# Attention and two MLPs on one core: transposes side by side, value products a step later, the exponentials' scale from a register

## The chip, the core and the metric

The kernel runs on one core of a Trainium2 chip. The core's engines run side by side, each through its own list of instructions in the order in which the program gives them: TensorE (PE in the profile; its weight loads are PEld), VectorE (DVE), ScalarE (ACT), GpSimd (POOL), and the queue on SyncE (SP) that issues most DMAs. They wait for each other by semaphores alone. The metric is the device time of one execution, in microseconds (us); all times below are us unless marked ns.

## The reference

What is computed is an attention over 2 batches, 12 heads, 448 positions and 64 dimensions per head, with the scores capped, and then two MLPs over the 896 tokens:

```python
scores = scale * np.matmul(q, k.transpose(0, 1, 3, 2))
scores = cap * np.tanh(scores / cap)
scores = scores - np.max(scores, axis=-1, keepdims=True)
attn = np.exp(scores)
attn = attn / (np.sum(attn, axis=-1, keepdims=True) + 1e-09)
out = np.matmul(attn, v)
# x: [896, 768] from out; then twice x = g(x @ w_in) @ w_out, 768 -> 2048 -> 768,
# g is ELU in the first MLP and leaky ReLU in the second
```

All is float32, and cap is an input (30).

## The kernel before, in words

**Two stages.** The attention works on 12 pairs of heads (n = 0 to 11), one pair after the other. The MLPs follow: products of 128x448 tiles, L655 (into the hidden layer) and L763 (out of it), each float32 product made of three with operands split into a rounded part and a remainder. The weights of the MLPs come in by DMA in a raw form and are converted on ACT and DVE (L564 to L594), then split (L304 on ACT, L307 on DVE). The first weights are converted while the attention still runs.

**One pair.** SP loads the pair's keys, queries and values (nk, nq, nv, L331). PE transposes keys and queries (L349, four products with the identity each, into PSUM tiles ntk and ntq), and DVE copies them out (kT, L367; qT with the scale 1/(8 cap), L363). PE makes the scores in four chunks of 112 keys (sc n.0 to n.3, L380, both heads of a chunk at once, in two halves of the array's rows). ACT takes tanh of each chunk (L400) and then the exponential of two chunks at a time, in place (e n.0 and e n.1, 112x1792, L408). POOL adds the two chunks of each half (s n.0, s n.1, L417), and DVE adds the halves (L423). PE multiplies this by ones (sm, L519), so that the sums of the softmax stand in every row, and the exponentials by the values in four chunks (po, L505, the two heads in two halves of the array's columns). DVE takes the reciprocal of the sums (rec, L525) and multiplies (xf, L533); ACT rounds xf (xh, L304), DVE takes the remainder (xl, L307), and both go into the first MLP.

**The exponential before** has two operands that are a column of 128 numbers in SBUF: the scale capb (the cap) and the bias nbound (minus its absolute value). The sums divide the bias out again. There is a second form of the block for large caps (row_softmax); a branch chooses at the start, and with this cap the first form runs.

**Buffers.** PSUM has eight banks: two score buffers of two banks (tag sc), one for transposes (nt), two for the products with the values (po, later also for the MLPs' accumulators), one for the sums (sm). Before the change ntk and ntq of every pair share the one nt buffer, apart from the first queries, which take sm.

**What sets the order.** Nothing is ordered by hand. Each step is put down with an engine, an assumed cost, what it reads and writes, and a wished or due time (`plan(...)`). The class `Plan` then plays the program through with these costs and writes down an order for each engine; PE pays `SWITCH` in that play when the kind of its work changes (transpose, scores, attend, MLP), and keeps to a kind a while. The order that comes out is fixed at build time. TP is the length that the plan assumes for one pair, and the wished times are multiples of it.

Of the kernel before, what the change touches and what calls it, by code (L numbers as in the profile page):

```python
# [23 lines left out]
class Plan:  # L24
# [10 lines left out]
    LANDING = 2.0  # L35
    AHEAD = 60.0
    STAY = 2.0
    SWITCH = 0.12

    def __init__(self, capacity):  # L40
        self.ops = []
# [151 lines left out]
@with_exitstack  # L193
def attention_elu_mlp_leaky_mlp(
    ctx: ExitStack,
    tc: tile.TileContext,
    q: bass.AP,
    k: bass.AP,
    v: bass.AP,
    cap: bass.AP,  # L200
    w_in1: bass.AP,
    w_out1: bass.AP,
    w_in2: bass.AP,
    w_out2: bass.AP,
    out: bass.AP,
):

    nc = tc.nc
    const = ctx.enter_context(tc.tile_pool(name="const", bufs=1))
    P, D = 128, q.shape[3]
    capb = const.tile([P, 1], F32, name="capb")
    nc.gpsimd.dma_start(out=capb, in_=cap.rearrange("(o n) -> o n", o=1).to_broadcast([P, 1]))

    first = {}
    for nm, src in (("k", k), ("q", q)):
        first[nm] = const.tile([src.shape[2] // 4, 4, 2, D], F32, name=f"first{nm}")  # L230
        nc.sync.dma_start(out=first[nm], in_=src[0, 0:2].rearrange("j (p c) d -> p c j d", c=4))

    busy = const.tile([P, P], F32, name="busy")
    nc.vector.memset(busy, 0.0)
    with tc.tile_pool(name="early", bufs=1, space=PSUM) as early:
        t = early.tile([P, P], F32, name="unused")
        for _ in range(IDLE_PRODUCTS):
            nc.tensor.matmul(t, busy, busy, start=True, stop=True)  # L238
    ident = const.tile([P, P], F32, name="ident")
    make_identity(nc, ident)  # L240
    ones = const.tile([P, D], F32, name="ones")
    nc.gpsimd.memset(ones, 1.0)
    third = const.tile([P, 1], F32, name="third")
    nc.vector.memset(third, -15.5 / 32.0)  # L244
    bits = nc.values_load(cap.bitcast(I32).rearrange("(o n) -> o n", o=1))
    ncap, nbound, qscale = (const.tile([P, 1], F32, name=x) for x in ("ncap", "nbound", "qscale"))
    scratch = const.tile([P, 1], F32, name="scratch")
    consts = dict(busy=busy, first=first, scratch=scratch, third=third, ident=ident, ones=ones, ncap=ncap, capb=capb, nbound=nbound, qscale=qscale)
    args = (tc, consts, q, k, v, w_in1, w_out1, w_in2, w_out2, out)
    with tc.If((bits & 0x7FFFFFFF) <= CAP_BOUND_BITS, preferred_fallthrough_block=True) as small:  # L250
        block(*args, bounded=True)
    with small.Else():
        block(*args, bounded=False)
# [3 lines left out]
def block(ctx, tc, consts, q, k, v, w_in1, w_out1, w_in2, w_out2, out, bounded):  # L257
# [49 lines left out]
        nc.vector.tensor_tensor(out=lo, in0=x, in1=hi.bitcast(F32), op=SUB)  # L307


    TP = 9.0  # L310
    NPAIR = len(order)
    TM = (NPAIR + 0.6) * TP

# [26 lines left out]
    def transpose_nat(nm, n, at):  # L340

        name, pt = f"{nm}T{n}", f"nt{nm}{n}"

        tag = "sm" if n == 0 and nm == "q" else "nt"

        def fn():
            t = tl("ps", tag, pt, [P, 512])
# [23 lines left out]
    def scores(n, c, at):  # L371
# [4 lines left out]
        def fn():  # L376
            t = tl("ps", "sc", name, [P, 2, 512])
            for j in range(2):
# [5 lines left out]
                    start=True, stop=True,  # L384
                )

        plan("PE", 0.93, fn, reads=[f"qT{n}", f"kT{n}"], writes=[(name, 0), (name, 1)],
             new={name: "sc"}, at=at, att=True, kind="scores")

    def half(n, h):  # L390
# [2 lines left out]
    def bounded_softmax(n):  # L393
        for c in range(NC):
# [10 lines left out]
                continue  # L405

            def exponent(name=name):
                nc.scalar.activation(V[name], V[name], AF.Exp, scale=capb[:CP], bias=nbound[:CP])  # L408

            plan("ACT", 1.8, exponent, reads=[(name, 0), (name, 1)],  # L410
                 writes=[(name, 0), (name, 1)], att=True)

            s = f"s{n}.{h}"
# [84 lines left out]
    def attend(n, c, at):  # L498
        po, e = f"po{n}", half(n, c // 2)

        def fn():
            if c == 0:
                tl("ps", "po", po, [P, 512])
            for j in range(2):
                nc.tensor.matmul(  # L505
                    V[po][j * D : (j + 1) * D, :S], V[f"nv{n}"][:, j, c], V[e][:, c % 2, j],
                    start=(c == 0), stop=(c == NC - 1),
                )

        plan("PE", 0.74, fn, reads=[(e, c % 2), f"nv{n}"], writes=[po],  # L510
             new={po: "po"} if c == 0 else None, at=at, att=True, kind="attend")

    def sums(n, at):
# [7 lines left out]
                    start=True, stop=True,  # L521
                )

        plan("PE", 0.74, fn, reads=[f"s{n}.0"], writes=[sm], new={sm: "sm"}, at=at, att=True, kind="attend")
        plan("DVE", 2.97, lambda: nc.vector.reciprocal(out=tl("att", "rec", rec, [P, S]), in_=V[sm][:, :S]),  # L525
             reads=[sm], writes=[rec], new={rec: "rec"}, att=True, due=at + 5)

# [367 lines left out]


    plan("ACT", 1.5, lambda: nc.scalar.activation(scratch, third, AF.Tanh), due=0.0)
    for n in range(NPAIR):
        T = (n + 0.3) * TP
        load("k", k, n)  # L900
        load("q", q, n)
        load("v", v, n)
        transpose_nat("k", n, T - 0.95 * TP)
        transpose_nat("q", n, T - 0.8 * TP)
        if n == 0:

            plan("PE", 0.4, lambda: idle_products("unusedq", 2), writes=["unusedq"], new={"unusedq": "po"},
                 at=T - 0.7 * TP, att=True)
        for c in range(NC):
            scores(n, c, T + c * TP / 4)  # L910
        (bounded_softmax if bounded else row_softmax)(n)
        for c in range(NC):
            attend(n, c, T + (c + 3.6) * TP / 4)
        if bounded:
            sums(n, T + 7.4 * TP / 4)
        x1(n, T + 2.6 * TP)
    TH = 6 * KM * MM
    TO = 3 * MS * (KF // 2) * MM
    T0 = TM
# [59 lines left out]
```

## Time and profile before

| | us |
|---|---|
| median of three runs (557.18 to 558.18) | 557.83 |
| the profiled execution, its own time | 557.47 |
| its span, first to last instruction | 555.6 |
| PE busy in it | 545.6 (98%) |
| DVE busy | 468.9 (84%) |
| ACT busy | 383.6 (69%) |
| POOL busy | 52.7 (9%) |
| attention, to the last product of sums | about 0 to 115 |
| MLPs | about 107 to 555 |

The profiled execution gives the durations; its own time is 557.47, of which 1.87 lie outside the span. A busy PE is not a PE at its peak: matmuls overlap, so the start of one matmul to the start of the next tells more than the duration of one. In the same way two neighbours on ACT or DVE overlap by some 0.1, and the step from start to start is what counts in a row of them. The chain of waits cuts the span into pieces that follow each other, and for these it gives what each cost. The granted clock of TensorE is 1.00 (2.4 GHz) in every stretch of the attention.

### The profile page before, as it was taken

The page shows a single profiled execution, that of the slowest core. Times are in us where ns is not written, and L with a number is a line of the kernel's source. Part 1 is how long each engine was busy: PE and PEld are TensorE (multiplying, and loading weights), DVE is VectorE, ACT ScalarE, POOL GpSimd, SP SyncE. Part 2 cuts the span into 40 slices and gives each one's busy share as a digit, 9 for nine tenths or more (in the row PEclk, how much of TensorE's full clock was granted, in tenths as well). Part 3 has the DMA queues.
Part 4 walks back from the last instruction along what each step waited for, and adds up shares of the span by engine and source line. Part 5 has one row for each costly group of instructions (what it writes and reads, how often), then busy time and mean ns, then how long its engine had stood idle before and what let it go on. Part 6 is the DMA issues. An engine that isn't in the chain of part 4 may idle for free.

```text
span 555.6 us, 7392 instructions
## 1 busy us (share of the span) xinstructions
PE 545.6 (98%) x2756; PEld 452.8 (81%) x2756; DVE 468.9 (84%) x606; ACT 383.6 (69%) x547; POOL 52.7 (9%) x32
## 2 busy tenths in 40 slices
PE   8999999999999999999999999999999999999995
PEld 5333333479999999999999999999999999999994
DVE  2699999996987899899999978987896499998662
ACT  5899999918977788865657757776665256665551
POOL 2554454500000000000000000000000000000000
PEclk9999999999999999999999999999999999999998
DMA  8833551145777677400012136677662000001112
GB/s 165 240 82 83 134 138 42 59 126 166 228 221 221 177 202 227 138 2 1 1 51 63 57 114 207 196 223 221 188 203 70 0 2 0 2 0 51 51 34 71
DMA packets 61434, 61.88 MB, mean 111 GB/s; under 512 B 23248, under 2 KB 53200, under 8 KB 61392
## 3 DMA queue, kind: packets, MB, share of 16 engines
q1 hardware_dynamic: 61120, 61.23, 38.8%
q8 instruction: 23, 0.38, 0.3%
q14 instruction: 19, 0.16, 0.1%
q10 hardware_dynamic: 240, 0.11, 0.1%
q0 software_dynamic: 32, 0.00, 0.0%
HBM read 58.59 MB, written 2.75 MB: 110 GB/s over the span
## 4 chain that ended last, share of the span: by engine, by line
PE 88%; DVE 5%; POOL 2%; ACT 2%; issue 2%; DVEq 0%; POOLq 0%; ACTq 0%
PE acc L655 29%; PE acc L763 24%; PE acs L763 12%; PE po L505 3%; DVE rec L525 2%; PE sm L519 1%; PE ct L848 1%; PE acs34.0_3866 L655 1%; PE acs31.0_3678 L655 1%; PE acs25.0_3299 L655 1%; PE acs22.0_3101 L655 1%; PE acs15.1_1848 L655 1%; PE acs12.1_1645 L655 1%; PE acs6.1_1253 L655 1%; PE acs28.1_3492 L655 1%
## 5 line engine op out<-in xcount | busy, mean ns | idle before, releaser
L525 DVE RECIPROCAL rec<-sm 128x448 f32<-128x448 f32 x12 | 35.4, 2954 | 2.2 <-PE sm L519 2.1
L367 DVE COPY kT<-ntk 128x448 f32<-128x448 f32 x12 | 7.4, 619 | 7.1 <-PE ntk L349 7.0
L349 PEld LDWEIGHTS ntq<-ident,nq 112*128 112x128 f32 x44 | 4.3, 140 | 9.3 <-DVE kT L367 8.6
L349 PEld LDWEIGHTS ntk<-ident,nk 112*128 112x128 f32 x44 | 4.3, 140 | 7.3 <-issue 6.7
L363 DVE TENSOR_SCALAR qT<-ntq,qscale 128x448 f32<-128x448 f32 x12 | 8.2, 679 | 1.5 <-PE ntq L349 1.5
L349 PE MATMUL ntq<-ident,nq 112*128 112x112 f32 x44 | 6.6, 273 | 1.4 <-DVE kT L367 1.4
L533 DVE TENSOR_TENSOR xf<-po,rec 128x448 f32<-128x448 f32 x12 | 7.5, 623 | 0.4
L576 ACT ACTIVATE rawo1.00.2_977<-rawo1.00.2_977 128x768 int32<-128x768 uint8 x1 | 0.9, 937 | 8.6 <-DMA rawo1.00.2_977<-in_moe_w_out_dram 8.6
L349 PE MATMUL ntk<-ident,nk 112*128 112x112 f32 x44 | 6.6, 273 | 0.0
L868 ACT COPY ob<-ct 112x512 f32<-112x512 f32 x7 | 4.1, 587 | 0.5
L238 PE MATMUL unused<-busy 128*128 128x128 f32 x14 | 3.4, 433 | 1.1 <-DVE third L244 1.1
L684 ACT ACTIVATE ea2.14.0_3936<-acs34.0_3866 128x448 f32<-128x448 f32 x1 | 0.5, 545 | 5.3 <-PE acs34.0_3866 L655 5.3
L832 ACT COPY c2.01.0_4934<-acc 128x448 f32<-128x448 f32 x1 | 0.5, 532 | 5.2 <-PE acc L763 5.2
L238 PEld LDWEIGHTS unused<-busy 128*128 128x128 f32 x14 | 3.1, 330 | 1.1 <-DVE third L244 1.1
L687 DVE TENSOR_TENSOR gg2.14.0_3940<-ea2.14.0_3936,acs34.0_3866 128x448 f32<-128x448 f32 x1 | 0.6, 622 | 3.9 <-ACT ea2.14.0_3936 L684 3.9
L834 DVE COPY c2.01.1_4942<-acc 128x448 f32<-128x448 f32 x1 | 0.6, 625 | 3.7 <-ACT c2.01.0_4934 L832 3.7
L307 DVE TENSOR_TENSOR tl2.1.3_3986<-gg2.3.0_3266,th2.1.3_3984 128x448 fp32r<-128x448 f32 x1 | 0.6, 624 | 3.6 <-PE acs L763 3.6
L304 ACT CAST th2.1.3_3984<-gg2.3.0_3266 128x448 fp32r<-128x448 f32 x1 | 0.6, 567 | 4.5 <-PE acs L763 4.5
L400 ACT ACTIVATE e0.0_160<-sc0.0_152 112x896 f32<-112x896 f32 x1 | 0.9, 919 | 3.9 <-PE sc0.0_152 L380 3.9
L669 ACT ACTIVATE ea1.0.0_1067<-acc 128x448 f32<-128x448 f32 x1 | 0.5, 546 | 4.4 <-PE acc L655 4.4
L675 DVE SCALAR_TENSOR_TENSOR gg1.0.0_1079<-ea1.0.0_1067,acc 128x448 f32<-128x448 f32 x1 | 0.6, 624 | 3.4 <-ACT ea1.0.0_1067 L672 3.4
L684 ACT ACTIVATE ea2.13.0_3886<-acc 128x448 f32<-128x448 f32 x1 | 0.5, 545 | 3.9 <-PE acc L655 3.9
(4966 smaller groups left out, 2237.2 us busy)
## 6 DMA issues: line engine op xcount, KB each, us to landing
nv<-in_v_dram SPq DMA_DIRECT2D x12, 224.0 KB, 2.9
nk<-in_k_dram SPq DMA_DIRECT2D x11, 224.0 KB, 3.2
nq<-in_q_dram SPq DMA_DIRECT2D x11, 224.0 KB, 3.9
out_dram<-ob SPq DMA_DIRECT2D x3, 672.0 KB, 4.4
rawg1.0_208<-in_moe_w_in_dram SPq DMA_DIRECT2D x1, 768.0 KB, 6.3
rawg1.1_253<-in_moe_w_in_dram SPq DMA_DIRECT2D x1, 768.0 KB, 5.9
rawg1.2_287<-in_moe_w_in_dram SPq DMA_DIRECT2D x1, 768.0 KB, 6.4
rawo1.00.0_519<-in_moe_w_out_dram SPq DMA_DIRECT2D x1, 768.0 KB, 5.5
```

Source lines behind the costliest of these rows:

```text
L238: nc.tensor.matmul(t, busy, busy, start=True, stop=True)
L349: nc.tensor.matmul(t[:, c * CP : (c + 1) * CP], V[f"n{nm}{n}"][:, c], ident[:CP, :CP], is_transpose=True, start=True, stop=True,)
L363: nc.vector.tensor_scalar(out=t, in0=V[pt][:, :S], scalar1=qscale, scalar2=None, op0=ALU.mult)
L367: nc.vector.tensor_copy(t, V[pt][:, :S])
L505: nc.tensor.matmul(V[po][j * D : (j + 1) * D, :S], V[f"nv{n}"][:, j, c], V[e][:, c % 2, j], start=(c == 0), stop=(c == NC - 1),)
L519: nc.tensor.matmul(t[j * D : (j + 1) * D, :S], ones[:CP], V[f"s{n}.0"][:, j], start=True, stop=True,)
L525: plan("DVE", 2.97, lambda: nc.vector.reciprocal(out=tl("att", "rec", rec, [P, S]), in_=V[sm][:, :S]), reads=[sm], writes=[rec], new={rec: ...
L533: nc.vector.tensor_tensor(out=tl("att", "xf", xf, [P, S]), in0=V[po][:, :S], in1=V[f"rec{n}"], op=ALU.mult)
L655: nc.tensor.matmul(bank(where[b]), V[g + w][:, kt, :], V[f"{part}{nm}.{b}.{kt}"], start=(x == 0 and i == 0), stop=(x == KM - 1 and i == 2),)
L763: nc.tensor.matmul(bank(where[m]), V[sp][:, kt % 2, m * P : (m + 1) * P], V[tp], start=(opens and kt == 0 and i == 0), stop=(kt == KF // 2 ...
L848: nc.tensor.matmul(t[:CP, x * P : (x + 1) * P], V[name][:, x * CP - a : (x + 1) * CP - a], ident, is_transpose=True, start=True, stop=True,)
L868: nc.scalar.copy(dst, src)
```

## The change

The transposes of a pair's keys and queries are asked for right after each other, between the second and the third chunk of scores of the pair before. For that the queries' transpose gets another PSUM buffer (tag po instead of nt). The products with the values and the sums of pair n are asked for after all four score chunks of pair n+1, instead of between them. The exponential takes its scale from a register, into which ACT loads the cap at the start, and has no bias; its values are larger by the factor e^|cap| for it, which the division by the sums takes out. Some assumed costs of the plan change too (SWITCH 0.12 to 0.17, scores 0.93 to 0.75, exponential 1.8 to 1.62, TP 9.0 to 8.3); they change nothing on the chip but the order.

```diff
-    SWITCH = 0.12
+    SWITCH = 0.17
...
+    consts["cap_register"] = nc.scalar.to_reg(bits)
...
-    TP = 9.0
+    TP = 8.3
...
-        tag = "sm" if n == 0 and nm == "q" else "nt"
+        tag = "nt" if nm == "k" else "sm" if n == 0 else "po"
...
-        plan("PE", 0.93, fn, reads=[f"qT{n}", f"kT{n}"], writes=[(name, 0), (name, 1)],
+        plan("PE", 0.75, fn, reads=[f"qT{n}", f"kT{n}"], writes=[(name, 0), (name, 1)],
...
             def exponent(name=name):
-                nc.scalar.activation(V[name], V[name], AF.Exp, scale=capb[:CP], bias=nbound[:CP])
-
-            plan("ACT", 1.8, exponent, reads=[(name, 0), (name, 1)],
+                nc.scalar.activation(V[name], V[name], AF.Exp, scale=consts["cap_register"])
+
+            plan("ACT", 1.62, exponent, reads=[(name, 0), (name, 1)],
...
-    for n in range(NPAIR):
+    def take(n):
         T = (n + 0.3) * TP
         load("k", k, n)
         load("q", q, n)
         load("v", v, n)
-        transpose_nat("k", n, T - 0.95 * TP)
-        transpose_nat("q", n, T - 0.8 * TP)
+        transpose_nat("k", n, T - 0.8 * TP)
+        transpose_nat("q", n, T - 0.75 * TP)
...
+    def give(n):
+        T = (n + 1.3) * TP
+        if bounded:
+            sums(n, T + 0.5 * TP)
         for c in range(NC):
-            scores(n, c, T + c * TP / 4)
+            attend(n, c, T + (0.6 + 0.1 * c) * TP)
+        x1(n, T + 1.3 * TP)
+
+    take(0)
+    for n in range(NPAIR):
+        T = (n + 0.3) * TP
+        for c in range(2):
+            scores(n, c, T + 0.1 * c * TP)
+        if n + 1 < NPAIR:
+            take(n + 1)
+        for c in range(2, NC):
+            scores(n, c, T + (0.1 + 0.1 * c) * TP)
         (bounded_softmax if bounded else row_softmax)(n)
-        for c in range(NC):
-            attend(n, c, T + (c + 3.6) * TP / 4)
-        if bounded:
-            sums(n, T + 7.4 * TP / 4)
-        x1(n, T + 2.6 * TP)
+        if n > 0:
+            give(n - 1)
+    give(NPAIR - 1)
```

How the order comes out shows best in the middle of the attention. On PE before, from the second chunk of scores of pair 6 on (ntk and ntq are the transposes of pair 7, po_528 the products of pair 5, po_600 those of pair 6; e5.1 is the second half of pair 5's exponentials; x4 is two chunks of two heads):

```order
L380 MATMUL sc6.1_544<-qT_507,kT_491 112x448 x2
L349 MATMUL ntk_551<-ident,nk_425 128x112 x4
L505 MATMUL po_528<-e5.1_515,nv_438 64x448 x4
L349 MATMUL ntq_569<-ident,nq_450 128x112 x4
L380 MATMUL sc6.2_577<-qT_507,kT_491 112x448 x2
L380 MATMUL sc6.3_589<-qT_507,kT_491 112x448 x2
L519 MATMUL sm_594<-s5.0_517,ones 64x448 x2
L505 MATMUL po_600<-e6.0_547,nv_542 64x448 x4
L380 MATMUL sc7.0_609<-qT_582,kT_563 112x448 x2
```

On PE now, from the first chunk of scores of pair 7 on (ntk and ntq are pair 8's, po_644 is pair 6's):

```order
L381 MATMUL sc7.0_595<-qT_569,kT_567 112x448 x2
L381 MATMUL sc7.1_602<-qT_569,kT_567 112x448 x2
L350 MATMUL ntk_607<-ident,nk_490 128x112 x4
L350 MATMUL ntq_613<-ident,nq_500 128x112 x4
L381 MATMUL sc7.2_621<-qT_569,kT_567 112x448 x2
L381 MATMUL sc7.3_628<-qT_569,kT_567 112x448 x2
L520 MATMUL sm_635<-s6.0_581,ones 64x448 x2
L506 MATMUL po_644<-e6.0_538,nv_531 64x448 x4
L506 MATMUL po_644<-e6.1_574,nv_531 64x448 x4
L381 MATMUL sc8.0_659<-qT_638,kT_633 112x448 x2
```

The products that stood between the two transposes are gone from there, and all four chunks of a pair's products follow its sums. A pair's run through PE changes its kind of work four times where it did six times; from the first transpose to the point where PE's list is the MLP's alone there are 59 such changes where there were 80.

On DVE before, from the reciprocal of pair 5 to that of pair 6 (ntk_621 and ntq_639 are pair 8's; g1.0l is a part of the first MLP weights):

```order
L525 RECIPROCAL rec_607<-sm_594 128x448
L533 TENSOR_TENSOR xf_627<-po_528,rec_607 128x448
L367 COPY kT_633<-ntk_621 128x448
L423 TENSOR_TENSOR s6.0_584<-s6.0_584,s6.1_614 112x896
L307 TENSOR_TENSOR g1.0l<-wg1.0_401,g1.0h 128x768
L363 TENSOR_SCALAR qT_657<-ntq_639,qscale 128x448
L307 TENSOR_TENSOR xl1.1.2_673<-xf_627,xh1.1.2_651 128x448
L525 RECIPROCAL rec_678<-sm_666 128x448
```

On DVE now, from the reciprocal of pair 6 to that of pair 7 (ntk_671 and ntq_677 are pair 9's, xl1.1.2 is pair 5's remainder):

```order
L526 RECIPROCAL rec_647<-sm_635 128x448
L534 TENSOR_TENSOR xf_664<-po_644,rec_647 128x448
L308 TENSOR_TENSOR xl1.1.2_682<-xf_600,xh1.1.2_624 128x448
L424 TENSOR_TENSOR s7.0_642<-s7.0_642,s7.1_657 112x896
L368 COPY kT_698<-ntk_671 128x448
L364 TENSOR_SCALAR qT_700<-ntq_677,qscale 128x448
L308 TENSOR_TENSOR xl1.0.3_707<-xf_664,xh1.0.3_690 128x448
L526 RECIPROCAL rec_714<-sm_702 128x448
```

A remainder has moved ahead of the addition of the halves, and the two copies of the transposes now stand behind that addition.

On SP before, behind the branch (nk_129 and nq_148 are pair 1's, nv_155 is pair 0's):

```order
L331 DMA nk_129<-in_k_dram 112x8x64
L331 DMA nq_148<-in_q_dram 112x8x64
L331 DMA nv_155<-in_v_dram 112x2x256
L331 DMA nk_162<-in_k_dram 112x8x64
L331 DMA nq_170<-in_q_dram 112x8x64
```

On SP now:

```order
L332 DMA nk_129<-in_k_dram 112x8x64
L332 DMA nq_145<-in_q_dram 112x8x64
L332 DMA nk_155<-in_k_dram 112x8x64
L332 DMA nq_162<-in_q_dram 112x8x64
L332 DMA nv_175<-in_v_dram 112x2x256
```

The first values have moved behind the keys and queries of pair 2; the loads of the first MLP weights have moved back by two places each, and from pair 4 on each pair's three loads stand in a row.

## Rows read from the trace of the kernel before

**Rows 1.** What PE waited for in the attention: total, times, longest.

```profile
PE ntq L349 <- DVE kT L367: 1.4, 3, 0.7
```

**Rows 2.** Chain of waits over pair 6: start, length, what.

```profile
56.55 0.94 PE sc6.0_539 L380 x4
57.49 0.75 PE sc6.1_544 L380 x4
58.24 0.53 PE ntk L349 x4
58.78 1.65 PE po L505 x8
60.43 0.53 PE ntq L349 x4
60.96 0.94 PE sc6.2_577 L380 x4
61.90 0.75 PE sc6.3_589 L380 x4
62.66 0.90 PE sm L519 x4
63.56 1.50 PE po L505 x8
65.06 0.96 PE sc7.0_609 L380 x4
```

**Rows 3.** Timeline of PE: start, length, instructions; the first queries' transpose.

```profile
5.36 0.55 PE L349 MATMUL ntq<-ident,firstq 112*128 112x112 f32 x4
5.74 0.62 PE L338 MATMUL unusedq<-busy 128*128 128x128 f32 x4
```

**Rows 4.** Busy time by stretch, columns as the first line says.

```profile
core 0: us, PE busy (x) PEld busy (x) DVE busy (x) ACT busy (x) POOL busy (x), PEclk, DMA share, GB/s
...
82.03:91.28 9.25, 8.57 (x46) 3.31 (x44) 9.22 (x8) 9.05 (x10) 4.19 (x3) 1.00 0.25 89
...
200.00:300.00 100.00, 100.00 (x500) 93.42 (x499) 95.78 (x141) 69.16 (x114) 0.00 (x0) 1.00 0.26 78
```

**Rows 5.** Timeline of ACT: a tanh, the exponential behind it, a rounding.

```profile
49.41 0.91 ACT L400 ACTIVATE e5.0_479<-sc5.1_476 112x896 f32<-112x896 f32 x1
50.36 1.88 ACT L408 ACTIVATE e5.0_479<-e5.0_479,nbound,capb 112x1792 f32<-112x1792 f32 x1
52.15 0.55 ACT L304 CAST xh1.1.1_509<-xf 128x448 fp32r<-128x448 f32 x1
```

**Rows 6.** Timelines of DVE over a pair, and of POOL in it.

```profile
55.15 2.95 DVE L525 RECIPROCAL rec<-sm 128x448 f32<-128x448 f32 x1
58.14 0.62 DVE L533 TENSOR_TENSOR xf<-po,rec 128x448 f32<-128x448 f32 x1
58.68 0.62 DVE L307 TENSOR_TENSOR xl1.1.1_557<-xf,xh1.1.1_509 128x448 fp32r<-128x448 f32 x1
...
59.75 1.08 DVE L423 TENSOR_TENSOR s5.0_517<-s5.0_517,s5.1_537 112x896 f32<-112x896 f32 x1
60.75 0.56 DVE L571 TENSOR_SCALAR rawg1.1_253<-rawg1.1_253 128x768 int32<-128x768 int32 x1
61.22 0.68 DVE L363 TENSOR_SCALAR qT<-ntq,qscale 128x448 f32<-128x448 f32 x1
61.81 2.08 DVE L307 TENSOR_TENSOR xl1.0.2_598<-xf,xh1.0.2_580 128x448 fp32r<-128x448 f32 x1
63.82 0.96 DVE L585 SCALAR_TENSOR_TENSOR wg1.1_408<-wg1.1_408,rawg1.1_253 128x768 int32<-128x768 int32 x1
...
61.32 2.10 POOL L417 TENSOR_TENSOR s6.0_584<-e6.0_547 112x896 f32<-112x896 f32 x1 [2.76 <-DVE rawg1.1_253 L571]
```

**Rows 7.** The load of pair 1's queries, and PE's third score chunk.

```profile
L331 SPq DMA_DIRECT2D nq<-in_q_dram x1: 677/677/677, 5.2 to 5.2; - x1
...
DMA to landing us min/median/max: 4.2/4.2/4.2
...
8.91 1.01 PE L380 MATMUL sc0.2_172<-qT,kT 64*112 64x448 f32 x4
```

More of the change, by code (lines that the diff above doesn't have):

```diff
@@ L508, in fn @@
                 )
-        plan("PE", 0.74, fn, reads=[(e, c % 2), f"nv{n}"], writes=[po],
+        plan("PE", 0.75, fn, reads=[(e, c % 2), f"nv{n}"], writes=[po],
              new={po: "po"} if c == 0 else None, at=at, att=True, kind="attend")
@@ L522, in fn @@
                 )
-        plan("PE", 0.74, fn, reads=[f"s{n}.0"], writes=[sm], new={sm: "sm"}, at=at, att=True, kind="attend")
+        plan("PE", 0.75, fn, reads=[f"s{n}.0"], writes=[sm], new={sm: "sm"}, at=at, att=True, kind="attend")
         plan("DVE", 2.97, lambda: nc.vector.reciprocal(out=tl("att", "rec", rec, [P, S]), in_=V[sm][:, :S]),
```

## The prediction

> **What bounds the kernel now.** I read the busy times first. In the MLPs PE is busy without a gap (100.00 of 100.00 in [rows 4]), and the change alters nothing there, so what can move lies in the first 115 us. There, too, PE is hardly ever idle: its only repeated wait is ntq on the copy of the keys' transpose, three times, 1.4 in total [rows 1]. Both transposes share one PSUM buffer, so ntq cannot start before DVE has copied ntk out. So PE sets the end, and an engine beside it matters only where PE waits for it. DVE is the one to fear: in the pair with the longest wait it is busy 9.22 of 9.25, and ACT 9.05 [rows 4].
>
> The next view is the chain of waits over pair 6, which has no wait in it: 56.55 to 65.06, 8.51 [rows 2]. Not all of that is work. Two chunks of scores take 0.94 and 0.75: the first one behind another kind of product pays 0.19. Two chunks of po cost 1.50 behind sm, which is of the same form, but 1.65 behind a transpose: 0.15. The sums take 0.90 behind scores, where a chunk of the same size among its like takes 0.75: 0.15. A transpose takes 0.53 in the chain. Between full-array products at the start its neighbour begins 0.38 after it [rows 3], so it pays 0.15 as well. A pair is then 4 x 0.75 (scores) + 4 x 0.75 (po) + 0.75 (sums) + 2 x 0.38 = 7.51, and six changes of kind: 4 x 0.15 + 2 x 0.19 = 0.98. That makes 8.49, against 8.51 measured, so the prices hold together.
>
> **The change part by part.** *The order on PE.* ntk and ntq stand together, and po behind sm. Gone from each pair are the step from transpose to po (1.65 to 1.50) and the one into ntq (0.53 to 0.38): 0.30, so 8.21 per pair. Over the whole attention the order has 21 fewer changes: ten fewer transpose-to-attend, nine fewer attend-to-transpose, two fewer scores-to-transpose, one fewer transpose-to-scores, one more scores-to-attend. At the prices above: 10 x 0.15 + 9 x 0.15 + 2 x 0.15 + 0.19 - 0.15 = **3.19 gained**. All of it is on PE, hence on the path. If a second transpose behind a first still took 0.53, nine of the 0.15 would stay and the gain would be 1.84; I take 0.38, since rows 3 show the very same operation at that pace.
>
> *The queries' buffer.* ntq no longer waits for kT: the 1.4 of [rows 1] **are gained**. In its place ntq takes one of the two po buffers. ntq and po come in turn, so ntq n+1 gets the buffer that ntq n left a whole pair earlier, and po of pair n+1 the one of po n, which xf frees. xf follows rec by 2.99 (58.14 less 55.15 [rows 6]), and rec starts right behind the sums, which now stand before po: its 2.99 run beside the four chunks (3.00) that po needs anyway. The next po comes a period later. I cost it at nothing; it is late only if DVE is some 4 us late. The copies kT and qT are now needed only when the pair after starts, some 5.6 later: after sc n.2 and n.3 (1.69), sums (0.90) and four chunks (3.00).
>
> *The exponential.* The trace shows no exponential with a register. Its bound above is today's 1.88 if dropping the two columns saves nothing; below, a straight line through the tanh of 896 (0.91) and the rounding of 448 (0.55), neither of which has a column operand: 0.55 + 3 x 0.36 = 1.63 [rows 5]. I take 1.65, the tanh being the same kind of operation. From start to start today's exponential costs 52.15 - 50.36 = 1.79, the new one some 1.56. On ACT a pair costs four tanh (0.81 and, before the exponential, 50.36 - 49.41 = 0.95, twice each), two exponentials and a rounding (0.55): 4.07 + 2 x 1.56 = 7.19, or 7.65 with today's, without weight conversions. Against 8.21 both leave room, and for pairs 5 to 9 the new order puts no conversion on ACT at all. So this part has **no term of its own**; its cover is PE, and it gives ACT 1.0 to spare in place of 0.56. If that cover is gone, the rival on the register applies.
>
> *The loads.* On SP the values of pair 0 stand behind two more loads, which SP takes some 0.7 each to issue. They land about 1.4 later, but their first product now stands behind the first two score chunks of pair 1 and has moved back by more than that. What is late is something else: ntq of pair 1 now follows ntk of pair 1 directly, so PE comes to it at 8.91, where sc0.2 stood, while its load is issued at 5.2 and lands 4.2 later, at 9.4 [rows 7]. Behind ntq stand sc0.2 and all the rest of PE's list. **0.45 lost**, between 0 (ACT's first exponential is the next limit there, and it hides a part) and 0.7.
>
> *DVE.* A pair costs rec 2.99, xf 0.54, xl and kT together 1.07, addition 1.00, qT 0.59: 6.19, and some 0.9 of weight conversion. That fits into 8.21. But a remainder that runs into POOL's addition is held: xl took 2.01 at 61.81, where POOL added from 61.32 to 63.42, and 0.54 at 58.68, where POOL had just ended [rows 6]. With one held remainder the pair needs 7.66, with a conversion 8.6. So DVE has no room in some pairs. What is late next is the **sums of a pair**: they need the addition of the halves, and this needs POOL's second addition. ACT's 7.19 begin about 1.1 into a period, when the first scores are done, so the second half leaves ACT at 8.3, POOL adds for 2.1, and so it ends some 2.2 into the next period; the sums are wanted 4.3 in (1.69 + 0.91 for the transposes + 1.69). Of these 2.1 the addition takes 1.0 and a held remainder another 0.55, which leaves some 0.5; a conversion more (0.9) and PE waits about 0.4. Behind the sums stand po and the next pair's scores. Before pair 11 the new order puts four conversion steps and a remainder ahead of the last kT, some 3.6 of DVE time, and the last scores wait if one of these is held. Bounds: 0, and 3.5 if most such places go wrong (0.4 to 0.75 at four, 1.5 at pair 11). Nearest are the waits of today, 1.4 in all; I take **1.0 lost**, less than today since the queue before what PE wants is shorter.
>
> *The assumed costs* act by the order alone; in the MLPs the order stays what it was but for a few rows, and DVE's list behind the last reciprocal holds the same steps. Nothing.
>
> **The sum.** 557.47 - 3.19 - 1.4 + 0.45 + 1.0 = 554.3 on the profiled execution. The median of the runs lies 0.36 above it, so **554.7**.
>
> **The rivals.** *All fits.* If no new wait appears (and the 0.45 is hidden), the sum is 557.83 - 4.6 = 553.2. For it: PE's waits today are few, though DVE is just as full. Against it: seven of the first nine remainders were held, like the one of 2.08 in [rows 6]. 15%.
>
> *DVE takes the place of the copy.* If nearly every pair has a held remainder and a conversion, DVE's pair is 8.6 as above, PE's 8.21 is not reached, and the pairs run at some 8.5 as before: the 3.19 go and only part of the 1.4 stays, 556.7 to 557.6. For it: DVE's 9.22 of 9.25 in [rows 4]. Against it: conversions can slip behind the attention, and the new order has moved several there. The Trainium skill has a rule for this (SBUF — State Buffer, "Who interferes with whom"): VectorE with two inputs in SBUF and GpSimd reading SBUF share a read port, and whoever starts first keeps it for the whole instruction. The rows of xl agree, 2.01 against 0.54. By that rule the change gives this rival's time wherever it puts a remainder into POOL's 2.1, and the new order does so behind nearly every xf. 17%.
>
> *The register is slow.* No row prices it. ACT's pair is 4.07 and two exponentials; it equals PE's 8.21 at 2.07 from start to start and today's 8.51 at 2.22. If reading a register cost 0.5 on top of 1.79, 2.29, the pair would be 8.65 on ACT, conversions not counted, and with 0.9 of these in half the pairs some 9.0 on average: 0.5 more than today's 8.51 over eleven pairs is 5.5, less the 1.4, and the end comes 4 later, **slower**, 562. The point is 2.2. [...] ScalarE: Activation LUTs in the Trainium skill ("What ACT_TABLE_LOAD costs") gives 93 ns for each column operand and names no register; by it the exponential would take 1.88 - 0.19 = 1.70, which is an estimate and leaves the sum as it is. 6%.
>
> *The transposes don't gain.* If a second transpose pays the change anyway, 1.84 stand in place of 3.19 and the time is 556.0; counted with the forecast.
>
> **How the numbers follow.** Forecast, 553.6 to 556.2: 60%. All fits, 553.2 or a little under: 15%. DVE, 556.2 to 558: 17%. Register or another wait that makes it slower: 8%. The likeliest is 554.7. The range runs from 552.9 to 556.8: it leaves out the register and the worse half of the DVE case, and a little below. A measurement of this kernel tells about 0.2% from no change, 1.1. Faster than 556.7 are the first two and half of the third: 0.83. Within 1.1: most of the other half, 0.11. Slower than 558.9: 0.06.
>
> **What would show it.** In the chain over a middle pair: sc to sc 8.2, ntk and ntq together 0.91, po 3.0 behind sm. In PE's waits: none on kT; some of 0.3 to 0.7 by sums on the addition L424, one by ntq on a load near 9. Exponentials of 1.63 to 1.70, with ACT idle 1.0 a pair where no weights stand. The last sums at some 111.4 instead of 114.5, and nothing changed behind. I am wrong if the chain shows DVE through the middle pairs (the DVE rival), if ACT is busy all through (the register), or if ntk and ntq together take 1.06.

## The result and the profile after

The changed kernel takes **553.06 us** (median of six runs, 552.48 to 553.31) against 557.89 for the kernel before beside it (557.01 to 558.62): a ratio of 0.9913 [0.9901, 0.9924]. That is 4.8 us faster, in the predicted direction, 1.6 below the predicted 554.7 and just inside the range. The profiled execution took 553.05 (span 551.2), so the comparison of the two profiles is one of 4.42 us.

The chain of waits over pair 7 answers [rows 2] (start, length, what):

```profile
61.44 0.94 PE sc7.0_595 L381 x4
...
63.13 0.53 PE ntk L350 x4
63.66 0.38 PE ntq L350 x4
64.05 0.94 PE sc7.2_621 L381 x4
...
65.74 0.90 PE sm L520 x4
66.64 3.01 PE po L506 x16
69.65 0.94 PE sc8.0_659 L381 x4
```

A pair is 8.21 from scores to scores, to the hundredth what the prediction worked out, and it is 8.21 in each of the pairs 5 to 9. The second transpose takes 0.38 behind the first. What PE waited for in the first 130 us (total, times, longest) answers [rows 1]:

```profile
PE sm L520 <- DVE s10.0_845 L424: 0.8, 1, 0.8
PE ntq L350 <- DMA nq<-in_q_dram: 0.5, 1, 0.5
```

No wait on the copy kT is left. There are two new ones, and only one of them is by the sums. The busy times by stretch, over the pair from 77.79 and over the same 100 us of the MLPs, answer [rows 4] (columns as there); an exponential and the rounding behind it on ACT answer [rows 5]:

```profile
77.79:86.00 8.21, 8.21 (x47) 3.40 (x45) 7.92 (x7) 7.09 (x9) 4.19 (x2) 1.00 0.45 124
200.00:300.00 100.00, 100.00 (x502) 93.75 (x501) 95.38 (x142) 69.83 (x117) 0.00 (x0) 1.00 0.25 75
```

```profile
47.82 1.70 ACT L409 ACTIVATE e5.0_475<-e5.0_475 112x1792 f32<-112x1792 f32 x1
49.43 0.55 ACT L305 CAST xh1.1.1_507<-xf 128x448 fp32r<-128x448 f32 x1
```

PE is busy all of 8.21, ACT has 1.1 to spare, DVE only 0.3. The exponential went from 1.88 to 1.70. On DVE one step of each of these pairs is still held by POOL, as in [rows 6], here the weight step L586 (2.22, from 62.15, while POOL adds until 63.55); but the addition of the halves behind it ends at 65.4, before the sums want it:

```profile
62.15 2.22 DVE L586 SCALAR_TENSOR_TENSOR wg1.0_391<-wg1.0_391,rawg1.0_237 128x768 int32<-128x768 int32 x1
64.30 1.08 DVE L424 TENSOR_TENSOR s6.0_581<-s6.0_581,s6.1_593 112x896 f32<-112x896 f32 x1
...
61.47 2.08 POOL L418 TENSOR_TENSOR s6.1_593<-e6.1_574 112x896 f32<-112x896 f32 x1 [0.87 <-PE po L506]
```

**Where the 4.42 lie.** Two marks cut both executions into three parts: the last sums, and the end of PE's last product. On PE's timelines, first before, then after:

```profile
114.54 0.97 PE L519 MATMUL sm<-s11.0_916,ones 112*64 112x448 f32 x4
548.32 0.42 PE L848 MATMUL ct012.0_4965<-ident,c2.01.2a 128*112 128x128 f32 x2
...
111.30 0.92 PE L520 MATMUL sm<-s11.0_920,ones 112*64 112x448 f32 x4
544.75 0.42 PE L849 MATMUL ct012.0_4965<-ident,c2.01.2a 128*112 128x128 f32 x2
```

The attention gives 3.24 (114.54 less 111.30), the MLPs 0.33 (433.78 and 433.45 between the starts of these two rows), and the stretch from the last product to the end of the span 0.83 (6.86 and 6.03). The forecast had 3.14, 0 and 0 for these (3.14 is 3.19 + 1.4 - 0.45 - 1.0).

### The profile page after: what moved, and what is told of

Read it like the earlier page. It is cut to its first block, busy times and chain, and to the rows that moved or that the text cites. A ratio compares the mean times of both kernels' runs of the same rounds, so it can differ in the third digit from the quotient of the medians.

```text
span 551.2 us, 7395 instructions
## 1 busy us (share of the span) xinstructions
PE 542.1 (98%) x2756; PEld 453.6 (82%) x2756; DVE 463.6 (84%) x606; ACT 379.3 (69%) x547; POOL 54.4 (10%) x32
## 3 DMA queue, kind: packets, MB, share of 16 engines
HBM read 58.59 MB, written 2.75 MB: 111 GB/s over the span
## 4 chain that ended last, share of the span: by engine, by line
PE 93%; DVE 4%; DMA 1%; SPq 1%; issue 0%; ACT 0%; DVEq 0%
PE acc L656 29%; PE acc L764 24%; PE acs L764 12%; PE po L506 5%; PE sm L520 2%; DVE rec L526 1%; PE ct L849 1%; PE ntk L350 1%; DMA nq<-in_q_dram 1%; PE ntq L350 1%; PE acs34.1_3867 L656 1%; PE acs28.1_3492 L656 1%; PE acs25.1_3300 L656 1%; PE acs22.1_3102 L656 1%; PE acs15.1_1845 L656 1%; PE acs12.1_1646 L656 1%
```

## The experiments

"Scores to sums" is the time from the first scores to the last sums, "MLPs" that from there to the end of the last product, "end" that from there to the end of the span, all in the profiled execution. Each ratio is to runs of the kernel before on the same chip, whose median there was 557.15 to 557.89. So the medians of two rows can differ by some 0.7 without a difference between the kernels, and for small differences the columns from the profiles say more. The changed kernel's two rows also differ: in the first execution PE waited 0.55 for a load, in the second not. The orders of the engines are the same as in the kernel that is changed, unless said.

| | median | ratio to before | scores to sums | MLPs | end |
|---|---|---|---|---|---|
| before | 557.89 | | 107.86 | 434.20 | 6.86 |
| before, again | 557.46 | 1.0000 [0.9991, 1.0009] | 107.82 | 434.16 | 6.87 |
| b_exp: new exponential | 555.73 | 0.9972 [0.9962, 0.9983] | 106.52 | 434.20 | 6.31 |
| b_buf: other bank | 557.02 | 0.9994 [0.9985, 1.0003] | 107.33 | 434.17 | 6.35 |
| b_exp_buf: both | 556.00 | 0.9978 [0.9969, 0.9988] | 106.58 | 434.18 | 6.38 |
| after | 553.06 | 0.9913 [0.9901, 0.9924] | 104.62 | 433.87 | 6.03 |
| after, again | 553.22 | 0.9925 [0.9911, 0.9939] | 104.11 | 433.86 | 5.79 |
| a_oldexp: old exponential | 555.14 | 0.9957 [0.9944, 0.9971] | 105.71 | 433.90 | 6.55 |
| a_nt: one bank | 562.23 | 1.0092 [1.0076, 1.0107] | 113.92 | 433.89 | 5.90 |
| a_apart: transposes apart | 555.74 | 0.9974 [0.9965, 0.9983] | 106.89 | 433.86 | 6.07 |
| a_split: products apart | 555.81 | 0.9971 [0.9960, 0.9982] | 106.37 | 433.87 | 5.98 |
| a_ends: waits mended | 554.21 | 0.9949 [0.9935, 0.9963] | 105.11 | 433.88 | 5.94 |
| a_pair: two pairs at once | 556.81 | 0.9989 [0.9980, 0.9998] | 106.65 | 433.87 | 6.50 |
| a_late: sums later | 552.37 | 0.9910 [0.9896, 0.9923] | 103.20 | 433.91 | 6.01 |

**The exponential alone, in the kernel before (b_exp).**

```diff
+    consts["cap_register"] = nc.scalar.to_reg(bits)
...
-                nc.scalar.activation(V[name], V[name], AF.Exp, scale=capb[:CP], bias=nbound[:CP])
+                nc.scalar.activation(V[name], V[name], AF.Exp, scale=consts["cap_register"])
```

> The kernel before with the new exponential alone (scale from a register, no bias), every engine's order as before. Theory (ScalarE is covered by TensorE, which bounds the attention): the exponential falls from 1.88 to 1.70 us, and the time stays within 0.3 us of the kernel before (557.6 to 557.9); the sums of the last pair end at 115.5, as before. Rival (ScalarE shares the path, and the part of the gain that the forecast lacks comes from it): 24 exponentials x 0.18 = up to 4.3 us shorter, in any case more than 1 us. For the end of the program, where one execution of before took 6.9 us from the last product's end to the span's end and one of after 6.0: if that is chance, it lies anywhere between here; if it belongs to the order of before, it is 6.9 again.

It is 1.7 us faster, and the scores to sums are 1.34 shorter: the theory was wrong, though ScalarE is not the bound, and the rival, which asked for more than 1, holds. What PE waited for in b_exp says how it came about:

```profile
PE ntq L350 <- DVE kT L368: 0.3, 1, 0.3
```

Of the 1.4 of [rows 1] only 0.3 is left, although both transposes still share their bank. One of the vanished waits, in pair 2, shows the way. First DVE and POOL in the kernel before, then in b_exp:

```profile
24.15 1.09 DVE L423 TENSOR_TENSOR s1.0_248<-s1.0_248,s1.1_266 112x896 f32<-112x896 f32 x1 [0.33 <-POOL s1.1_266 L417]
...
22.03 2.09 POOL L417 TENSOR_TENSOR s1.1_266<-e1.1_246 112x896 f32<-112x896 f32 x1 [1.44 <-ACT e1.1_246 L408]
```

```profile
24.62 1.08 DVE L424 TENSOR_TENSOR s1.0_248<-s1.0_248,s1.1_266 112x896 f32<-112x896 f32 x1
...
22.27 2.09 POOL L418 TENSOR_TENSOR s1.1_266<-e1.1_246 112x896 f32<-112x896 f32 x1 [1.23 <-ACT e1.1_246 L409]
```

Before, DVE came to the addition and stood 0.33 until POOL had added the second half, which POOL could start only when the exponential was done; and kT stood behind that addition in DVE's list. With the shorter exponential POOL ends at 24.36, before DVE is there at 24.62, and nothing stands still. The path is exponential, POOL, addition, kT, ntq. In pair 5 another one led to kT: before, the remainder xl1.1.0 had to wait for ACT's rounding, which stood behind an exponential, and from there (35.71) to kT (50.43) DVE worked without a gap; in b_exp that remainder starts 0.2 earlier after the first scores of pair 3, and the next one, which POOL holds, takes 1.91 in place of 2.16. None of it shows as a busy ScalarE.

**The other bank alone, in the kernel before (b_buf).**

```diff
-            t = tl("ps", tag, pt, [P, 512])
+            t = tl("ps", "sm" if nm == "q" else tag, pt, [P, 512])
```

> The kernel before with one thing changed: the queries' transposes go to the accumulator bank of the sums, which is free then, and not to the one that the keys' transposes use; every engine's order as before. Theory (the waits for the keys' copy cost 1.4 us and nothing takes their place): TensorE's waits on the copy kT go from 1.4 to 0, and the kernel is 1.0 to 1.4 us faster (556.5). Rival (the wait moves on: the next scores wait for the queries' copy, or the bank of the sums is still held by the reciprocal): same time as before, with as much waiting on qT or on the reciprocal.

0.4 us faster by the median, with an interval that includes no change, and 0.53 in scores to sums. The waits on kT are gone, and others stand in their place:

```profile
PE sm L519 <- DVE qT L363: 0.5, 1, 0.5
PE sc11.0_865 L380 <- ACT e10.1_856 L400: 0.3, 1, 0.3
```

The first belongs to this experiment: the sums wait until the queries have left their bank. The second is ScalarE's, tanh late before the last pair. So both were partly right, and the 1.4 was no term of the bank alone.

**The old exponential in the changed kernel (a_oldexp).** The edit is that of b_exp, backwards.

> The changed kernel with the exponential as it was (scale and bias from columns), every engine's order as in the changed kernel. Theory (ScalarE has 1.1 us to spare in a pair of 8.21): exponentials of 1.88, ScalarE's idle time in a pair falls to 0.7, the pair stays at 8.21, and the time is 0 to 0.5 us longer than the changed kernel (553.1 to 553.6). Rival (the exponential carries part of the gain): 1 to 4 us longer, with TensorE's waits on tanh or the exponential. End of the program from the last product: 6.0 if it belongs to the changed order, anywhere between 6.0 and 6.9 if it is chance.

1.9 to 2.1 us slower by the medians. The pairs were not all 8.21 any more, and PE waited for tanh, which the changed kernel never does, once more for 0.2 beside the two shown, and longer for the sums of pair 10:

```profile
PE sm L520 <- DVE s10.0_845 L424: 1.2, 1, 1.2
...
PE sc4.2_424 L381 <- ACT e4.0_407 L401: 0.4, 1, 0.4
...
PE sc2.2_284 L381 <- ACT e2.0_267 L401: 0.2, 1, 0.2
```

The rival is right, in size near its lower end. In pairs 6 to 9 ScalarE still stands idle for 0.6 to 0.9, and pairs 6 and 8 stay at 8.21; pairs 7 and 9 are 8.34, since the sums start (66.56 in pair 7) right when the addition that a conversion delayed ends (66.51). The waits for tanh fall in the first five pairs, where ScalarE, late from the start, has 0.2 at most from pair 1 on (in pair 3 it has 0.18, with the new exponential 0.75 to 1.18). An average over the pairs doesn't show that.

**Queries behind keys in one bank (a_nt).**

```diff
-            t = tl("ps", tag, pt, [P, 512])
+            t = tl("ps", "nt" if n and bounded else tag, pt, [P, 512])
...
```

> The changed kernel with the queries' transposes back in the one bank of the keys' (the copy kT stands ahead of ntq, so that VectorE does it ahead of the addition of halves in some pairs); TensorE's order as in the changed kernel. Theory (the new order needs the second bank: queries right behind keys wait for the whole copy): each of 11 pairs waits 0.6 to 1.3 us on kT, the pair goes from 8.21 to 8.9 or 9.5, and the kernel is 6 to 14 us slower than the changed one (559 to 567), so slower than before. Rival (the waits of the old kernel were small, 1.4 in all, and stay so): 0 to 1.5 us slower than the changed kernel.

9.0 to 9.2 us slower than the changed kernel and slower than before, with the two waits at the lower end of what was expected: 7.9 in 11.

```profile
PE ntq L350 <- DVE kT L368: 7.9, 11, 0.7
...
69.28 0.63 DVE kT L368
...
69.95 0.60 PE ntq L350 x4
```

The first line is of the waits, the others of the chain over pair 7. A pair is 9.14, 0.93 more than 8.21: 0.72 of wait, and ntq takes 0.60 where it took 0.38. So the new order needs the second bank, and here a wait of PE costs 0.22 more than its length. In the kernel before it cost little more: there ntq stood behind another kind anyway, and pair 5, with a wait of 0.42, took 9.00 in place of 8.51.

**Transposes apart, products apart (a_apart, a_split).** Here and below `move` takes an instruction out of the finished order and puts it ahead of another (behind it, with True); `opens` finds the one that writes a tile first.

```diff
     order_of_issue = plan.order()
...
+        for n in range(3, NPAIR):
+            move(opens[f"ntk{n}"], opens[f"sc{n - 1}.1"])
```

> The changed kernel with keys and queries transposed apart again in 9 stretches: the keys' transposes stand one chunk of scores earlier, so that each of these pairs has two changes of kind more. Theory (a change of kind costs TensorE 0.15 to 0.19 us, and nothing hides it): 18 changes, the pair goes from 8.21 to 8.55, and the kernel is 2.7 to 3.2 us slower than the changed one. Rival (the new order gains by its fewer waits, and a change of kind costs nothing by itself): the pair stays at 8.2 to 8.25, and the time within 0.5 us.

```diff
     order_of_issue = plan.order()
...
+        for n in range(2, 9):
+            move(opens[f"po{n}"], opens[f"sc{n + 1}.3"])
```

> The changed kernel with the products with the values apart in 7 stretches: the first chunk's two products of the pair before stand ahead of the last chunk of scores, which makes two more changes of kind each. Theory (each change of kind costs 0.15 to 0.19, with the products as with the transposes): pairs of 8.55, and 2.1 to 2.7 us slower than the changed kernel (555.3 to 555.9). Rival one (only the transposes carry the price): pairs of 8.2 to 8.3. Rival two (the last scores come 1.1 us later, and ScalarE with 1.1 to spare hands that on through the additions to the sums): pairs over 8.8, over 4 us slower.

Both cost some 2.6 us against the two medians of the changed kernel (2.5 to 2.7 and 2.6 to 2.75), a_apart at or just under the lower end of what was expected, a_split at the upper. By the profiles a_apart is 2.8 and a_split 2.3 longer from scores to sums than the changed kernel's second execution, which like them had no wait for the load. The chain over pair 7, a_apart first, then a_split:

```profile
62.95 0.94 PE sc7.0_595 L381 x4
63.89 0.53 PE ntk L350 x4
64.43 0.94 PE sc7.1_607 L381 x4
65.37 0.53 PE ntq L350 x4
...
71.50 0.56 PE sc8.0_659 L381
```

```profile
66.44 0.90 PE po L506 x4
67.34 0.94 PE sc7.3_631 L381 x4
```

Each pair is 8.55 in both (71.50 less 62.95 in a_apart): two changes more cost 0.34, one step from 0.38 to 0.53 or 0.75 to 0.90, and one from 0.75 to 0.94. The price is the same with transposes and with products, nothing hides it in these pairs, where PE waits for nothing, and the 1.1 by which a_split delays the last scores goes nowhere. The theory of the order holds, twice.

**All but the order (b_exp_buf).** The edits of b_exp and b_buf together.

> The kernel before with the new exponential and the queries' transposes in the sums' bank, the order of every engine as before: all of the change but the order. What is left to the changed kernel is the order alone. Theory (21 fewer changes of kind at 0.15 to 0.19, less the two new waits of 0.55 and 0.82 that the changed kernel has): from the first scores to the last sums 106.0 to 106.3 us (the two profiles of the changed kernel: 104.6 and 104.1; before 107.9; new exponential alone 106.5), so that the order is worth 1.4 to 2.2; time 555.2 to 555.6. Rival (the order is worth less than the changes of kind say, since the exponential and the bank already bring most): 105.0 or below, and 554.2 or less.

106.58 and 556.0, some 0.3 above what the theory gave, and nowhere near the rival. The 0.3 is a wait of its own, before the scores of pair 11:

```profile
PE sc11.0_865 L381 <- DVE qT L364: 0.3, 1, 0.3
```

From there to the changed kernel are 1.96 and 2.47 in its two executions. Adding back the changed kernel's waits (0.55 + 0.82 in the first, 0.82 alone in the second) gives 3.33 or 3.29, and without the wait of b_exp_buf (0.35 on PE's timeline) the order itself is worth 2.98 or 2.94; the forecast had 3.19.

**The waits mended by order (a_ends, a_late).**

```diff
     order_of_issue = plan.order()
...
+        move(opens["ntk1"], opens["sc0.2"], True)
+        move(opens["ntq1"], opens["ntk1"], True)
...
+        move(half10, merge)
...
+        move(opens["sm10"], first)
```

> The changed kernel with its two waits of TensorE mended by order alone: the third chunk of pair 0's scores stands ahead of pair 1's transposes (whose load came 0.55 late), and the last but one addition of halves stands ahead of the conversion that held VectorE 2.85 us, with the sums of pair 10 ahead of the first products of the MLP, which also takes two changes of kind away. Theory: -0.5 at the start, -0.8 and -0.3 at the end, 1.3 to 1.6 us faster than the changed kernel (551.5 to 551.8). Rival (the waits move on: scores wait for tanh at the start, the last sums of pair 11 or the next conversion at the end): 0 to 0.5 us faster.

1.0 to 1.2 us *slower* than the changed kernel. There is no wait for the load, but that doesn't show that the move hid it: the first scores came at 7.17 here, and a_late (6.88) and a_oldexp (7.04) had no such wait in the old place either. Scores waited 0.3 for tanh; and at the other end the wait of the sums grew from 0.8 to 1.4. DVE in the changed kernel, where POOL adds from 99.74 to 102.40:

```profile
100.37 2.85 DVE L595 SCALAR_TENSOR_TENSOR wg1.2_841<-rawg1.2_322,wg1.2_841 128x768 int32<-128x768 int32 x1
103.15 1.08 DVE L424 TENSOR_TENSOR s10.0_845<-s10.0_845,s10.1_867 112x896 f32<-112x896 f32 x1
```

DVE and POOL in a_ends, and the wait:

```profile
100.67 2.98 DVE L424 TENSOR_TENSOR s10.0_845<-s10.0_845,s10.1_867 112x896 f32<-112x896 f32 x1
103.56 0.94 DVE L595 SCALAR_TENSOR_TENSOR wg1.2_841<-rawg1.2_322,wg1.2_841 128x768 int32<-128x768 int32 x1
...
100.03 2.66 POOL L418 TENSOR_TENSOR s11.0_923<-e11.0_872 112x896 f32<-112x896 f32 x1 [1.98 <-ACT e11.0_872 L409]
...
PE sm L520 <- DVE s10.0_845 L424: 1.4, 1, 1.4
```

In the changed kernel the conversion L595 took 2.85 there and the addition 1.08; moved ahead of it, the addition takes 2.98 and the conversion 0.94. It is the place that is held, from POOL's start, and not the instruction. The Trainium skill says just this (SBUF — State Buffer, "Who interferes with whom": the engine that issues second is blocked for the whole instruction of the first), and these rows agree. A cure has to put something else on PE:

```diff
     order_of_issue = plan.order()
...
+        second = [o for o in order_of_issue if o["engine"] == "PE" and "g1.0h" in o["uses"]][1]
+        move(second, opens["sm10"])
...
+            move(o, behind, True)
```

> The changed kernel with the second group of products of the MLP (six, 1.2 us) ahead of the sums of pair 10, so that TensorE works while VectorE is held, and with the last addition of halves right behind the reciprocal of pair 10. Theory (the held instruction stays held, but TensorE needs its result later): the wait of 0.8 us on s10 goes to 0, the last sums come 0.6 to 0.8 us earlier, and the time is 0.6 to 0.8 us less than the changed kernel's (552.3 to 552.6). Rival (VectorE's chain of addition, reciprocal, addition ends at the same time, as it did where the addition was moved): the wait turns up at the last sums, 0 to 0.2 us.

The wait is gone, and scores to sums take 103.20, 0.91 less than in the changed kernel's second execution, which had no wait for the load either. The time is 552.37, 0.7 and 0.85 below the two medians of the changed kernel, as the theory has it; but the runs (551.85 to 552.58 and 552.07 to 553.48) overlap, and so do the ratios to before (0.9910 against 0.9913 and 0.9925), so that the gain in the whole time is not shown. PE in a_late works through and comes to the sums when DVE is done:

```profile
104.26 0.97 PE L520 MATMUL sm<-s10.0_845,ones 112*64 112x448 f32 x4
...
110.08 0.92 PE L520 MATMUL sm<-s11.0_920,ones 112*64 112x448 f32 x4
```

The last sums start 1.22 earlier than the changed kernel's, of which 0.33 were there before pair 11 already (its first scores start at 94.21 and 94.54). This version has the lowest median and the shortest stretch from scores to sums.

**Fewer changes still (a_pair).**

```diff
...
     order_of_issue = plan.order()
...
+            for x in (f"ntk{n}", f"ntq{n}"):
+                move(opens[x], opens[f"ntq{n - 1}"] if x[2] == "k" else opens[f"ntk{n}"], True)
...
```

> The changed kernel with the transposes of two pairs at a time in four places (pairs 4 and 5, 6 and 7, 8 and 9, 10 and 11): 16 transposes in a row, and none in the stretch after it, so eight changes of kind fewer. The second pair's keys go to the sums' bank, and their copies stand in other buffers. Theory (price of a change of kind 0.15 to 0.19): stretches of 9.1 and 7.5 in turn, and 1.2 to 1.4 us faster than the changed kernel (551.7). Rival (VectorE's four copies in a row, 2.4 us, hold up the addition of halves, and the sums wait 0.3 to 1.0 in four to eight pairs): from 0.5 faster to 3 us slower.

3.6 to 3.75 us slower than the changed kernel, a little over the rival's end. PE's waits:

```profile
PE sm L525 <- DVE kT L373: 2.1, 2, 1.0
...
PE sc4.2_428 L386 <- ACT e4.0_421 L406: 0.3, 1, 0.3
```

In all four stretches without transposes the third chunk of scores waited 0.3 for tanh to free a score buffer; the transposes had filled just that gap. The wait cost more than its length here too: the chunk behind it took 1.01 where one behind its like takes 0.75. In two of the others the sums waited 1.0 for their bank, since DVE's copies came late behind a held conversion. The transposes between the second and the third chunk do more than save changes: they give ScalarE time.

**Both kernels again.**

> The changed kernel once more, as it is, to see what of its gain is the same in a second execution. From the first scores to the last sums of pair 11 it took 104.6 us, and from there to the last product 433.9 (before: 107.9 and 434.2); these have one order and should repeat within 0.1. The start (first transposes to first scores, 1.97 in both kernels' profiles) and the end (last product to the end of the span, 6.0 against 6.9) hold no changed instruction: if they are chance, they come out elsewhere in 1.9 to 3.0 and 5.9 to 6.9, as in the four kernels run so far; if the end belongs to the changed kernel, it is 6.0 again.

> The kernel before once more, as it is: what of it repeats. From the first scores to the last sums 107.9, from there to the last product's end 434.2, both within 0.2. The end of the program (last product to the end of the span) was 6.9 in its first execution, 6.3 and 6.4 in two kernels with its order, 5.8 to 6.6 in seven with the changed one: by chance it comes out in 5.8 to 6.9; at 6.9 again it would belong to this kernel.

Attention and MLPs repeat, apart from the 0.51 by which the second execution of the changed kernel is shorter between scores and sums. That is the wait for the load: its first scores came 0.96 later, and the queries had landed by then. The end was 6.87 again before and 5.79 after.

## Why the prediction was right, and where not

**The bound, the pair, the order: right.** 8.21 per pair as forecast and the last sums at 111.30 for some 111.4, the second transpose at 0.38, the price of a change 0.15 to 0.19 in two doses, 2.9 to 3.0 for the order against 3.19. The rival by which the transposes don't gain is out, and DVE did not become the bound of the middle pairs.

**The wait of 1.4 and the exponential: the step that failed.** The prediction gave the exponential no term, since ScalarE had room, and gave the bank all of the 1.4. Alone in the old order the exponential brought 1.34, the bank 0.53 (with 0.8 of new waits of its own) and both 1.28 (with 0.35), so they take away the same waits; in the new order, without the exponential, 1.1 to 1.6 by the profiles (1.6 against the execution without the wait for the load) and some 2.0 by the medians would be lost. That ScalarE had 0.56 to spare in a pair covers its throughput. It does not cover the path from one exponential through POOL and DVE to the copy or the sums. In the sum the two errors cancel, by luck: both edits together give 1.28, not far from 1.4. The length of the exponential, 1.65, was a little off too: it is 1.70, and 1.61 from start to start. The Trainium skill's figure (ScalarE: Activation LUTs, "What ACT_TABLE_LOAD costs": two column operands less) had given 1.70 as an estimate, and the trace agrees.

**The new waits.** One, of 0.82, where 1.0 was forecast over several places. The mechanism was the named one, a conversion held by POOL ahead of the addition, but only at pair 10. In the middle pairs the addition ended in time, though a step of DVE was held in each; with the old exponential two of these pairs take 0.13 more and the waits come to 2.0, so the shorter exponential helped here too. The load cost 0.55 (0.45 forecast) in one execution of the changed kernel and nothing in the other.

**Behind the attention: not forecast.** "Nothing" was wrong by 0.33 in the MLPs. All nine profiled executions with the new order have 433.86 to 433.91, all five with the old one 434.16 to 434.20. On PE and DVE, before and then after:

```profile
276.90 0.47 PE L763 MATMUL acc<-tl1.4.4_2464,S1.4.2h 128*128 128x448 f32 x1
276.23 0.62 DVE L307 TENSOR_TENSOR tl1.4.4_2464<-gg1.4.1_1307,th1.4.4_2457 128x448 fp32r<-128x448 f32 x1
...
273.46 0.36 PE L764 MATMUL acc<-tl1.4.4_2461,S1.4.2h 128*128 128x448 f32 x1
271.58 0.61 DVE L308 TENSOR_TENSOR tl1.4.4_2461<-gg1.4.1_1313,th1.4.4_2455 128x448 fp32r<-128x448 f32 x1
```

Before, the remainder ended at 276.85 and PE began with it at 276.90, 0.14 later than its pace; after, it was done 1.3 ahead. Across this place the lead grows by 0.26. So the 0.33 goes with the plan's order, of which the prediction called the few other rows in the MLPs nothing; which of these rows does it, no run shows.

**The rest of the 1.6 missed:** 0.36 is the step from the profiled execution to the median, which the kernel before had and this one did not; 0.83 is the end; 0.33 the MLPs, and 0.10 the attention. With these the time came out where the rival "all fits" had it (553.2), but not by that rival's way: it has no new wait, and the changed kernel's profile has two, of 0.55 and 0.82. What makes the end shorter stays open. The instructions are the same. The last store's issue (SP's timeline, before and after) is 1.59 long before and 0.89 after, and the data land 4.7 and 3.6 after its start (4.3 and 3.4 in the second executions):

```profile
549.63 1.59 SPq L876 DMA_DIRECT2D out_dram<-ob01.2_4968  x1
...
546.37 0.89 SPq L877 DMA_DIRECT2D out_dram<-ob01.2_4968  x1
```

Over all profiled executions the end lies between 5.8 and 6.9, below 6.1 in seven of nine with the new order and above 6.3 in all five with the old. It repeated in both kernels, but a_oldexp and a_pair, which have the new order, end at 6.55 and 6.50; whether the 0.83 belongs to the change is not shown.

## What to carry to other kernels

Spare time of an engine in a pair covers its throughput, not its latency: before an edit is costed at nothing, follow its result to the engine that sets the end, step by step, and look for a wait that it feeds. Two edits that remove the same wait don't add up, and terms of a sum should be priced with the others in place. A change of kind on PE has a price that holds wherever PE never waits; more of them can be saved only as long as the piece between was not the time in which another engine caught up.

## What the runs showed of the hardware

The start was not the same in every execution. The first transposes begin at 4.71 or 4.72 in all but one (4.55), but take from 0.57 to 0.98, so that the first scores come anywhere from 6.56 to 7.67. PE in the changed kernel's second execution, and the busy times of that stretch:

```profile
4.72 0.98 PE L350 MATMUL ntk<-ident,firstk 112*128 112x112 f32 x4 [0.30 <-PE unused L238]
7.64 1.01 PE L381 MATMUL sc0.0_152<-qT,kT 64*112 64x448 f32 x4 [0.32 <-DVE qT L364]
...
5.00:7.00 2.00, 2.00 (x13) 2.00 (x12) 0.87 (x4) 0.00 (x0) 0.00 (x0) 1.00 0.52 118
```

In [rows 3] the first queries' transpose took 0.55; here it took 0.92. The granted clock reads 1.00 (2.4 GHz) in this stretch in both, so these rows don't show what halves the pace. And a wait of PE can cost more than its length: where the instruction behind it would have followed its like, it took 0.22 more (a_nt, a transpose, 0.60 for 0.38) or 0.26 more (a_pair, scores, 1.01 for 0.75); where it paid a change of kind anyway, 0.07 (the kernel before, 0.60 for 0.53).
